# A scheduled two-stage MLP kernel on one core: x0 and x1 joined in one load, single-tile groups up to tile 5, and another load, PE and helper order

## Chip, core and metric

The kernel runs on one core of a Trainium2 chip. The time is the device time of one execution in microseconds (us); lower is better. A core has a tensor engine (PE, with PEld for its weight loads), a vector engine (DVE), a scalar engine (ACT), GpSimd (POOL) and a sync engine (SP). DMAs are issued here from SP and from ACT, each with its own ring, and run on the core's 16 DMA engines.

## What is computed

x is one sequence of S = 2048 tokens with D = 512 channels, F is 1792, everything is bf16. From the reference:

```python
    h = _gelu(_layernorm(x, axis=-1) @ w1)
    c = D // 4
    g0 = jnp.pad(h[:, :, 0*c:1*c], ((0, 0), (1, 0), (0, 0)))[:, :S, :]
    g1 = jnp.pad(h[:, :, 1*c:2*c], ((0, 0), (0, 1), (0, 0)))[:, 1:, :]
    g2 = jnp.pad(h[:, :, 2*c:3*c], ((0, 0), (2, 0), (0, 0)))[:, :S, :]
    g3 = jnp.pad(h[:, :, 3*c:   ], ((0, 0), (0, 2), (0, 0)))[:, 2:, :]
    hs = jnp.concatenate([g0, g1, g2, g3], axis=-1) @ w2
    x1 = x + hs
    h2 = _gelu(_layernorm(x1, axis=-1) @ w3) @ w4
    return x1 + h2
```

The four quarters of h are shifted along the sequence by +1, -1, +2 and -2 tokens, so token tile t of hs needs h of tiles t-1, t and t+1.

## The kernel before, in words

The sequence is cut into 16 tiles of 128 tokens. Layer 1 normalises x and multiplies by w1 (`up1`), GELU puts h, transposed, into `hT`; `mix` multiplies four shifted slices of `hT` by w2 and DVE adds x to give x1. Layer 2 normalises x1, multiplies by w3 (`up2`), GELU gives `h2T`, and `down` multiplies by w4; DVE adds x1 and a DMA stores the tile. A layer-2 tile t carries the number q = 16 + t in the tables, so `ty:16` is the transposition of layer-2 tile 0.

A tile's normalisation (`ln`, lines 384 to 465) is a chain of small steps: statistics on DVE (`bnst`, line 416, and `bnag`, line 418) or, for the tiles in `STAT_ACT`, on ACT (`sum`, line 395, `ssq`, line 400, with `msq` and `vpe` on DVE, lines 408 and 412); then the reciprocal root on POOL (`rstd`, line 423); then the normalisation itself on the engine that `NORM` names (DVE, line 445; ACT, line 454; POOL, line 457; the last two need `nmr`, line 450, on the engine that `NMR` names). The normalised tile is then transposed, by PE for the tiles named `sa`, `sb`, `ty` in the script (line 490, with a copy from PSUM, line 498, on the engine that `EVAC` names) and by a DMA transpose from SP (line 463) for the other 24. Tile 0 goes another way (`NAT`): centred only, split into two halves, multiplied with the tokens as rows (`ra`, `rb`, line 528), GELU with the scale (line 569), and h transposed by PE (`th`, line 594) and copied by the engine in `HEV` (line 604).

`GROUPS` says how many neighbouring tiles one `up` step takes together: a group of n tiles streams n*128 columns for each weight block (`mm_up`, line 626, GELU at line 641). `mix` is line 666 with its residual at lines 673 and 677; `down` is line 695 with its residual at line 703.

What sets the order: PE executes `SCRIPT` from left to right, exactly. Loads are issued in the order of `LOADS`, an item marked `@act` on the ACT ring, all others on SP (lines 368 and 377; `x4-5` is one DMA for two tiles, `w1a` and `w1b` are the halves of w1; a `tp` item for a tile that PE transposes has no effect). All other work is put in order by the planner `Program.order` and `place`: it computes a due time for each operation back from the script, starting at `DUE`, adds `BIAS`, and simulates the engines and rings with fixed durations, `HOP` and `LAG`. Each engine then executes its list in order, so that a waiting instruction holds everything behind it on its engine. `y_ps` has three buffers, used in rotation by `up` and the PE transposes, `o_ps` has two, used by `mix`, `down`, `th` and the warm-up. Before anything has landed PE runs a number of matmuls on zeros (`warm`, line 720).

Of the kernel before, what the change touches and what calls it, by code (L numbers as in the profile page):

```python
# [25 lines left out]
class Program:  # L26
# [2 lines left out]

    HOP = {"pe": 200.0, "dve": 155.0, "act": 220.0, "pool": 120.0, "sp": 70.0}  # L30
    LOOK = {"dve": 300.0, "act": 300.0}
    DUE = 164483.0
    BEGIN = {"sp": 30.0, "act": 150.0, "pe": 400.0, "dve": 150.0, "pool": 450.0}
    ENTRY = 1900.0
    COLD, RESTART = 4300.0, 800.0
    LAG = {"load": 750, "tp": 700}

    def __init__(self):
        self.ops = []
# [12 lines left out]
    def order(self):  # L52
# [58 lines left out]
        assert seen == len(self.ops), "cycle"  # L111
        if self.DUE:

            topo, left = [], [len(d) for d in preds]
            stack = [i for i, n in enumerate(left) if n == 0]
            while stack:
                i = stack.pop()
                topo.append(i)
                for j in succs[i]:
                    left[j] -= 1  # L120
                    if left[j] == 0:
                        stack.append(j)
            due, t = {}, self.DUE
            for op in self.ops:
# [12 lines left out]
        for op in self.ops:  # L137
            op.prio += BIAS.get(op.name, 0.0)
            if op.first is not None:
# [11 lines left out]
    def place(self, succs, order_only):  # L151
# [46 lines left out]
        def land(op):  # L198
            nonlocal moved, last
            if op.queue == "tp":  # L200
                at = max(clock + 500.0, op.start + 2450.0, last + 600.0) + self.LAG["tp"]
            elif op.name.startswith("out"):
                at = clock + 300.0
                self.total = max(self.total, at)
            else:
                moved += op.dur
                at = clock + 600.0 + min(600.0, 0.3 * moved) + (600.0 if op.dur > 1400.0 else 0.0)
                at += self.LAG["load"] if moved > 1200.0 else 50.0
            if op.queue != "tp":
# [47 lines left out]
        self.seq = out  # L257
        return out

GROUPS = {1: (1, 1, 1, 1, 2, 1, 4, 2, 2, 1), 2: (2, 4, 4, 2, 4)}  # L260
NORM = {0: "act", 3: "act", 7: "pool", 8: "act", 9: "pool", 10: "pool", 11: "pool", 12: "pool", 14: "act", 15: "act", 16: "pool", 18: "act", 19: "act", 24: "pool", 25: "act", 26: "pool", 27: "pool", 29: "pool", 30: "pool", 31: "act"}
EVAC = {0: "both", 1: "both", 2: "both", 4: "both", 8: "both", 9: "dve", 10: "dve", 11: "dve", 12: "dve", 13: "dve", 14: "dve", 16: "dve", 17: "dve", 19: "both", 20: "both", 21: "both", 22: "both", 23: "both", 24: "dve", 25: "both", 27: "both", 29: "both", 30: "both", 31: "both"}
STAT_ACT = (0, 7, 9, 12, 13, 15, 18, 21, 25, 29, 30)
TAIL = (256, 160, 96)
NMR = {0: "pool", 1: "pool", 3: "pool", 5: "pool", 6: "pool", 7: "pool", 8: "pool", 9: "pool", 11: "pool", 13: "pool", 14: "pool", 15: "pool", 16: "pool", 17: "pool", 18: "pool", 20: "pool", 21: "pool", 22: "pool", 26: "pool", 27: "pool", 28: "pool", 29: "pool", 31: "pool"}
NAT = (0,)
SPLIT = (0,)
CSPLIT = ()
HEV = {0: "dve", 4: "dve"}
BIAS = {}  # L270
LOADS = """
x1 x2 tp2 x0@act w1a w1b x3 x4-5 tp5 w2a w2b x6-7 w3 tp17 w4a x8-10 w4b tp6 x11-12 tp1 tp16 x13-15
"""
SCRIPT = """
warm:9 sa:0 sb:0 ty:1 ra:0 rb:0 ty:2 up1:1 th:0 up1:2 mix:0 ty:3 ty:5 mix:1 ty:4 up1:3-4 ty:16 mix:2 ty:17
mix:3 up2:0 mix:4 up1:5 down:1 down:0 mix:5 up1:6-7 mix:8 mix:6 up1:9 mix:9-10 up1:8 mix:7 mix:11 up2:1
mix:13 mix:15 up2:3 down:5 mix:12 up2:2 mix:14 down:2 down:4 down:3 down:6-8 down:11 down:9 up2:4 down:10
down:12-15
"""

def bass_standalone__mixer_s_mlp__prompt_kernel(nc, x, w1, w2, w3, w4, out):
# [3 lines left out]
    NT, DC, FC = S // P, D // P, F // P  # L285
    groups = {l: [(sum(GROUPS[l][:i]), n) for i, n in enumerate(GROUPS[l])] for l in GROUPS}
    NXN, NO, NPAIR, NOB, NJ = 16, 4, 3, 2, 4
# [8 lines left out]
    with ExitStack() as es:  # L296
# [87 lines left out]
        def ln(layer, t):  # L384
# [3 lines left out]
            col = lambda a: a[:, q : q + 1]  # L388
            how = NORM.get(q, "dve")
            sign = -1.0 if q in NAT and how == "act" else 1.0  # L390
            if q in STAT_ACT:
                if layer == 1:
# [22 lines left out]
            else:  # L415
# [4 lines left out]
                       writes=[(("mv", q), 0), (("vpe", q), 0)], dur=75)  # L420
            var = vpe[:, q : q + 1] if q in STAT_ACT else mv[:, q, 1:2]
            pg.add("pool", f"rstd{q}",
# [3 lines left out]
            if q in NAT:  # L426
                assert how != "act" or q in STAT_ACT

# [18 lines left out]
            else:  # L447
                eng = NMR.get(q, "dve")
                pg.add(eng, f"nmr{q}",
# [17 lines left out]
        def pe_transpose(t, q, pair):  # L467
            layer = 1 if q < NT else 2
            how = EVAC.get(q, "act")
            if pair:  # L470
# [104 lines left out]
        def h_transpose(t):  # L575
            g = group_of[1, t]
            how = HEV.get(t, "act")
            k = NAT.index(t)
# [71 lines left out]
        def mm_mix(t):  # L650
# [20 lines left out]
            wr = [(("x1", t), 0)]  # L671
            if NT + t in STAT_ACT:
                f = lambda e: e.scalar_tensor_tensor(x1_sb[:, t, :], dst, 1.0, x_sb[:, t, :], ALU.mult, ALU.add,  # L673
# [198 lines left out]
```

## Time and profile before

| | |
|---|---|
| time, median of 5 runs | 135.45 us (135.12 to 135.84) |
| the profiled execution | 135.84 us, of which the span of the trace is 134.5 us and 1.34 us lie around it |
| granted TensorE clock | 1.000 |
| busy share of the span: PE, PEld | 98%, 53% |
| busy share: ACT, DVE, POOL | 43%, 38%, 22% |
| chain that ended last | PE 94%, DMA 4%, SP's queue 1% |
| loads on SP (issue start, time to landing) | x1 0.1, 2.4; x2 0.6, 2.6; w1a 1.0, 4.8; w1b 1.5, 5.0; w4b 9.9, 11.5 |
| load on ACT | x0 0.2, 2.6 |
| DMA transposes | 24, median 1.27 us to issue, 2.5 us to landing |

The table of busy times tells how full an engine is over the whole span. The chain is read back from the last instruction: at each step it names what the step was waiting for, so it shows what set the time. The timeline gives start, duration, engine, line and operation; in brackets stands how long the engine had been idle and what ended that. Matmul durations in the timeline overlap, because matmuls are pipelined; the chain's pieces do not.

### The profile page before, as it was taken

To read this page: it belongs to the slowest core of one execution; us is meant where nothing else is said; L and a number is where in the kernel's file an instruction comes from. 1 tells how busy PE (TensorE), PEld (TensorE's weight loads), DVE (VectorE), ACT (ScalarE), POOL (GpSimd) and SP (SyncE) were. 2 spreads that over 40 slices of the span, in tenths; PEclk is the share of its full clock that TensorE was granted. 3 is DMA by queue.
4 is the path that set the end of the run, shared out by engine and by line. 5 is a ranking of instruction groups with operands and counts; after the bars stand their busy time and mean duration, and the time that the engine had idled before them with its cause. 6 is when DMAs were issued, how large, how long until landed. Compare 5 with 4: busy or idle time off the path is not lost.

```text
span 134.5 us, 2014 instructions
## 1 busy us (share of the span) xinstructions
PE 131.4 (98%) x789; PEld 71.4 (53%) x789; DVE 50.8 (38%) x134; ACT 58.4 (43%) x92; POOL 29.7 (22%) x68
## 2 busy tenths in 40 slices
PE   8799999999999999999999999999999999999994
PEld 3287687644666444478544444444444444444464
DVE  2689986856178930070061004232222200012222
ACT  5789349989544275547315554000000155520000
POOL 2444549892102860006010001200000000000000
DMA  4999999455452134100411000211111100001112
GB/s 134 301 386 396 350 299 239 90 80 115 82 116 78 34 73 95 39 0 1 82 39 39 0 0 0 70 47 44 39 39 57 60 0 0 0 5 39 39 39 78
DMA packets 21289, 12.19 MB, mean 91 GB/s; under 512 B 13856, under 2 KB 20768, under 8 KB 21280
## 3 DMA queue, kind: packets, MB, share of 16 engines
q1 hardware_dynamic: 20704, 11.80, 32.8%
q10 hardware_dynamic: 576, 0.26, 0.7%
q8 instruction: 6, 0.10, 0.3%
q14 instruction: 3, 0.02, 0.1%
HBM read 6.82 MB, written 2.10 MB: 66 GB/s over the span
## 4 chain that ended last, share of the span: by engine, by line
PE 94%; DMA 4%; SPq 1%; issue 0%; DVE 0%
PE y_ps L626 46%; PE o_ps L695 36%; PE o_ps L666 10%; DMA w_sb<-in_w_dram 4%; PE y_ps L490 1%; SPq L368 1%; PE y_ps L528 0%; SPq L377 0%; DVE o_sb L703 0%; PE o_ps L594 0%; SPq L857 0%
## 5 line engine op out<-in xcount | busy, mean ns | idle before, releaser
L626 PE MATMUL y_ps<-xnT,w_sb 128*128 128x512 bf16 (+2 forms) x424 | 63.6, 309 | 0.0
L626 PEld LDWEIGHTS y_ps<-xnT,w_sb 128*128 128x128 bf16 x424 | 38.3, 98 | 24.9
L641 ACT ACTIVATE h2T<-y_ps 128x1024 bf16<-128x1024 f32 (+1 forms) x29 | 28.6, 994 | 48.8 <-PE y_ps L626 48.6
L695 PE MATMUL o_ps<-w_sb,h2T 128*128 128x512 bf16 (+3 forms) x252 | 49.1, 355 | 0.0
L695 PEld LDWEIGHTS o_ps<-w_sb,h2T 128*128 128x128 bf16 x252 | 23.6, 98 | 24.7
L703 DVE TENSOR_TENSOR o_sb<-o_ps,x_sb 128x512 bf16<-128x512 f32 (+3 forms) x18 | 11.4, 632 | 46.9 <-PE o_ps L695 46.9
L423 POOL TENSOR_TENSOR rstd<-mv,neghalf 128x1 f32<-128x1 f32 x21 | 11.5, 549 | 23.6 <-DVE mv L418 14.2
L666 PE MATMUL o_ps<-w_sb,hT 128*128 128x512 bf16 x64 | 15.8, 379 | 0.0
L416 DVE BATCH_NORM_STATS2 st<-x_sb 128x6 f32<-128x512 bf16 x21 | 14.1, 678 | 3.5 <-DMA x_sb<-in_x_dram 3.4
L423 POOL TENSOR_TENSOR rstd<-vpe,neghalf 128x1 f32<-128x1 f32 x11 | 6.0, 547 | 29.3 <-DVE vpe L412 29.2
L673 DVE SCALAR_TENSOR_TENSOR x_sb<-o_ps,x_sb 128x512 bf16<-128x512 f32 x5 | 3.4, 686 | 19.2 <-PE o_ps L666 19.2
L641 ACT ACTIVATE hT<-y_ps 128x512 bf16<-128x512 f32 (+1 forms) x10 | 8.1, 807 | 5.4 <-PE y_ps L626 5.3
L677 DVE TENSOR_TENSOR x_sb<-o_ps,x_sb 128x512 bf16<-128x512 f32 x11 | 7.6, 687 | 4.2 <-PE o_ps L666 4.0
L666 PEld LDWEIGHTS o_ps<-w_sb,hT 128*128 128x128 bf16 x64 | 6.0, 98 | 5.8
L457 POOL TENSOR_SCALAR xn_buf<-x_sb,rstd,nmr 128x512 bf16<-128x512 bf16 x11 | 8.4, 765 | 0.8 <-DVE nmr L450 0.4
L400 ACT ACTIVATE junk<-x_sb 128x512 bf16<-128x512 bf16 x11 | 6.9, 624 | 2.2 <-DVE x_sb L673 2.2
L454 ACT ACTIVATE xn_buf<-x_sb,nmr,rstd 128x512 bf16<-128x512 bf16 x8 | 6.3, 806 | 0.8 <-POOL nmr L450 0.7
L445 DVE TENSOR_SCALAR xn_buf<-x_sb,mv,rstd 128x512 bf16<-128x512 bf16 x12 | 5.3, 443 | 2.9 <-POOL rstd L423 2.6
L720 PE MATMUL o_ps<-zeros 128*128 128x512 bf16 x9 | 4.0, 626 | 0.4 <-DVE zeros L347 0.4
L395 ACT ACTIVATE junk<-x_sb 128x512 bf16<-128x512 bf16 x6 | 3.7, 624 | 0.7 <-DMA x_sb<-in_x_dram 0.7
L418 DVE BATCH_NORM_AGGREGATE mv<-st 128x2 f32<-128x9 f32 x21 | 3.8, 189 | 0.3
L450 POOL TENSOR_SCALAR nmr<-mv,rstd 128x1 f32<-128x1 f32 x13 | 3.4, 263 | 0.7
(34 smaller groups left out, 28.4 us busy)
## 6 DMA issues: line engine op xcount, KB each, us to landing
out_dram<-o_sb SPq DMA_DIRECT2D x15, 128.0 KB, 1.7
w_sb<-in_w_dram SPq DMA_DIRECT2D x1, 1792.0 KB, 10.0
w_sb<-in_w_dram SPq DMA_DIRECT2D x2, 896.0 KB, 11.7
w_sb<-in_w_dram SPq DMA_DIRECT2D x4, 256.0 KB, 5.2
x_sb<-in_x_dram SPq DMA_DIRECT2D x3, 256.0 KB, 5.2
x_sb<-in_x_dram SPq DMA_DIRECT2D x2, 384.0 KB, 9.1
x_sb<-in_x_dram SPq DMA_DIRECT2D x3, 128.0 KB, 2.6
xnT<-xn_buf SPq DMA_TRANSPOSE x24, 2.5
```

The costliest lines, as they stand in the source:

```text
L400: (lambda d: (lambda e: e.activation(d, src, ACT_F.Square, accum_out=sums[:, q, 1:2])))(junk[:, b, :]),
L416: pg.add("dve", f"bnst{q}", lambda e: e.bn_stats(st9[:, q, 0:6], src), reads=rs, writes=[(("st", q), 0)], dur=605)
L423: lambda e: e.tensor_tensor(col(rstd), var, neghalf[:], ALU.pow),
L445: lambda e: e.tensor_scalar(dst, src, mv[:, q, 0:1], rstd[:, q : q + 1], ALU.subtract, ALU.mult),
L454: f = lambda e: e.activation(dst, src, ACT_F.Identity, bias=nmr[:, q : q + 1], scale=rstd[:, q : q + 1])
L457: f = lambda e: e.tensor_scalar(dst, src, rstd[:, q : q + 1], nmr[:, q : q + 1], ALU.mult, ALU.add)
L626: ins = e.matmul(y_ps[:, p, W * i : W * (i + 1)], wsb[:, dc, P * fc : P * (fc + 1)], src[:, dc, P * t0 : P * t0 + W], start=(dc == 0), sto ...
L641: (lambda d, s: (lambda e: e.activation(d, s, ACT_F.Gelu_apprx_tanh)))(dst, ysrc),
L666: ins = e.matmul(dst, hT[:, j, c0 : c0 + P], w2_sb[:, j, :], start=(j == 0), stop=(j == DC - 1))
L677: f = lambda e: e.tensor_tensor(x1_sb[:, t, :], dst, x_sb[:, t, :], ALU.add)
L695: ins = e.matmul(dst, h2T[:, fc, P * t : P * (t + 1)], w4_sb[:, fc, cs], start=(fc == 0), stop=(fc == FC - 1))
L703: (lambda d, c: (lambda e: e.tensor_tensor(o_sb[:, oi, c], d, x1_sb[:, t, c], ALU.add)))(dst, cs),
```

## The change

It touches tables only; no function is altered. x0 and x1 become one DMA on SP, and ACT issues no load. Layer-1 groups before: tiles 0, 1, 2, 3 alone, 4-5, 6 alone, 7-10, 11-12, 13-14, 15 alone. After: tiles 0 to 5 alone, 6-9, 10 alone, 11-12, 13 alone, 14-15. One warm-up matmul is added. The loads after x4-5 come in another order, most of x as single tiles, and no DMA transpose stands between loads. The tables of engines for the helpers, the planner's `DUE`, `LAG` and `BIAS`, and the order of PE's script are others.

```diff
-    DUE = 164483.0
+    DUE = 94375.3
...
-    LAG = {"load": 750, "tp": 700}
+    LAG = {"load": 450, "tp": 700}
...
-GROUPS = {1: (1, 1, 1, 1, 2, 1, 4, 2, 2, 1), 2: (2, 4, 4, 2, 4)}
-NORM = {0: "act", 3: "act", 7: "pool", 8: "act", 9: "pool", 10: "pool", 11: "pool", 12: "pool", 14: "act", 15: "act", 16: "pool", 18: "act", 19: "act", 24: "pool", 25: "act", 26: "pool", 27: "pool", 29: "pool", 30: "pool", 31: "act"}
-EVAC = {0: "both", 1: "both", 2: "both", 4: "both", 8: "both", 9: "dve", 10: "dve", 11: "dve", 12: "dve", 13: "dve", 14: "dve", 16: "dve", 17: "dve", 19: "both", 20: "both", 21: "both", 22: "both", 23: "both", 24: "dve", 25: "both", 27: "both", 29: "both", 30: "both", 31: "both"}
-STAT_ACT = (0, 7, 9, 12, 13, 15, 18, 21, 25, 29, 30)
+GROUPS = {1: (1, 1, 1, 1, 1, 1, 4, 1, 2, 1, 2), 2: (2, 4, 4, 2, 4)}
+NORM = {0: "act", 4: "pool", 9: "pool", 11: "pool", 12: "pool", 13: "pool", 14: "pool", 15: "act", 19: "pool", 20: "pool", 21: "act", 22: "act", 23: "act", 25: "act", 28: "pool", 29: "act", 31: "act"}
+EVAC = {0: "dve", 2: "both", 3: "dve", 8: "both", 9: "dve", 10: "both", 11: "both", 13: "dve", 15: "dve", 16: "both", 17: "dve", 18: "dve", 20: "both", 22: "dve", 27: "both", 29: "both", 30: "dve", 31: "both"}
+STAT_ACT = (0, 5, 7, 8, 9, 13, 21, 22, 28, 30)
...
-HEV = {0: "dve", 4: "dve"}
-BIAS = {}
+HEV = {0: "dve", 1: "dve", 3: "dve", 4: "dve", 6: "dve"}
+BIAS = {"bnag14": -172.25, "bnag2": -591.918, "bnag28": -353, "bnst6": 1934.91, "msq0": -541.481, "ssq4": -586, "vpe0": -295.453, "vpe9": 895}
 LOADS = """
-x1 x2 tp2 x0@act w1a w1b x3 x4-5 tp5 w2a w2b x6-7 w3 tp17 w4a x8-10 w4b tp6 x11-12 tp1 tp16 x13-15
+x0-1 x2 w1a w1b x3 tp17 tp4 x4-5 w2b w2a x8 tp4 w3 tp17 x10 x9 tp1 x7 x6 w4a w4b x15 x12 x14 tp0 x11 x13
 """
 SCRIPT = """
-warm:9 sa:0 sb:0 ty:1 ra:0 rb:0 ty:2 up1:1 th:0 up1:2 mix:0 ty:3 ty:5 mix:1 ty:4 up1:3-4 ty:16 mix:2 ty:17
-mix:3 up2:0 mix:4 up1:5 down:1 down:0 mix:5 up1:6-7 mix:8 mix:6 up1:9 mix:9-10 up1:8 mix:7 mix:11 up2:1
-mix:13 mix:15 up2:3 down:5 mix:12 up2:2 mix:14 down:2 down:4 down:3 down:6-8 down:11 down:9 up2:4 down:10
-down:12-15
+warm:10 sa:0 sb:0 ty:1 ra:0 rb:0 ty:2 up1:1 th:0 up1:2 ty:3 mix:0 up1:3 mix:1 ty:4 mix:2 ty:5 up1:4 ty:16
+up1:5 ty:17 mix:3 up2:0 mix:4 down:1 up1:6 down:0 mix:5 up1:8 up1:7 mix:6-7 up1:9 mix:9 mix:8 up1:10 mix:10
+up2:1 mix:11 mix:15 up2:2 mix:12 down:2 down:4 mix:14 up2:3 mix:13 down:3 down:6-7 up2:4 down:10-11 down:8
+down:14 down:5 down:9 down:12-13 down:15
 """
```

`NMR` changes in the same manner (fewer entries on POOL); `TAIL`, the split of the last tile's `down` into 256, 160 and 96 columns, stays. What the planner makes of the tables, engine by engine, is fixed when the program is built: in the first 17 us DVE then runs `bnst3 ev2dve bnag3 bnst4 norm3 evh0 bnag4 msq5 ev3 vpe5 x1_0 bnst16 norm5 x1_1 bnag16 bnst17 norm16 bnag17 x1_2 norm17 ev16dve msq8 vpe8 ev17`, ACT runs `gelur0 ev2act sum5 gelu1_1 ssq5 gelu1_2 sum8 ssq8 gelu1_3 ev4 ev5 gelu1_4 ev16act sum7 gelu1_5`, and SP issues all loads and then `tp8 tp7 tp6 tp9 tp10 ...`. (`ev` is the copy of a transposed tile, `evh0` that of tile 0's h, `x1_t` the residual after `mix:t`, `gelu1_g` the GELU of `up1:g`.)

More of the change, by code (lines that the diff above doesn't have):

```diff
@@ L258, in place @@
         return out
-GROUPS = {1: (1, 1, 1, 1, 2, 1, 4, 2, 2, 1), 2: (2, 4, 4, 2, 4)}
-NORM = {0: "act", 3: "act", 7: "pool", 8: "act", 9: "pool", 10: "pool", 11: "pool", 12: "pool", 14: "act", 15: "act", 16: "pool", 18: "act", 19: "act", 24: "pool", 25: "act", 26: "pool", 27: "pool", 29: "pool", 30: "pool", 31: "act"}
-EVAC = {0: "both", 1: "both", 2: "both", 4: "both", 8: "both", 9: "dve", 10: "dve", 11: "dve", 12: "dve", 13: "dve", 14: "dve", 16: "dve", 17: "dve", 19: "both", 20: "both", 21: "both", 22: "both", 23: "both", 24: "dve", 25: "both", 27: "both", 29: "both", 30: "both", 31: "both"}
-STAT_ACT = (0, 7, 9, 12, 13, 15, 18, 21, 25, 29, 30)
+GROUPS = {1: (1, 1, 1, 1, 1, 1, 4, 1, 2, 1, 2), 2: (2, 4, 4, 2, 4)}
+NORM = {0: "act", 4: "pool", 9: "pool", 11: "pool", 12: "pool", 13: "pool", 14: "pool", 15: "act", 19: "pool", 20: "pool", 21: "act", 22: "act", 23: "act", 25: "act", 28: "pool", 29: "act", 31: "act"}
+EVAC = {0: "dve", 2: "both", 3: "dve", 8: "both", 9: "dve", 10: "both", 11: "both", 13: "dve", 15: "dve", 16: "both", 17: "dve", 18: "dve", 20: "both", 22: "dve", 27: "both", 29: "both", 30: "dve", 31: "both"}
+STAT_ACT = (0, 5, 7, 8, 9, 13, 21, 22, 28, 30)
 TAIL = (256, 160, 96)
-NMR = {0: "pool", 1: "pool", 3: "pool", 5: "pool", 6: "pool", 7: "pool", 8: "pool", 9: "pool", 11: "pool", 13: "pool", 14: "pool", 15: "pool", 16: "pool", 17: "pool", 18: "pool", 20: "pool", 21: "pool", 22: "pool", 26: "pool", 27: "pool", 28: "pool", 29: "pool", 31: "pool"}
+NMR = {0: "pool", 4: "pool", 5: "pool", 6: "pool", 7: "pool", 10: "pool", 14: "pool", 15: "pool", 16: "pool", 17: "pool", 18: "pool", 19: "pool", 20: "pool", 22: "pool", 25: "pool", 27: "pool", 28: "pool", 31: "pool"}
 NAT = (0,)
```

## The prediction

> **What bounds the kernel now.** I read the chain that ended last first. Its pieces are start, duration, what:
>
> ```profile
> 1.49 4.99 DMA w_sb<-in_w_dram
> 6.48 0.05 issue
> 6.53 0.60 PE y_ps L528 x2
> 7.13 0.22 PE y_ps L490 x4
> 7.36 0.89 PE y_ps L626 x16
> ...
> 9.39 0.94 PE o_ps L666 x4
> ...
> 24.58 6.04 PE o_ps L695 x28
> ...
> 117.53 15.19 PE o_ps L695 x98
> 132.72 0.02 issue
> 132.74 0.26 DVE o_sb L703
> ```
>
> The second half of w1 (`w1b`, issued at 1.49) lands at 6.48. From 6.53 to 132.72 every piece is PE with no gap between: 126.19 us of matrix work. After it come one DVE addition and the last store (134.5 − 132.72 = 1.8). The waits of PE say the same; columns are total, times, longest:
>
> ```profile
> PE y_ps L528 <- ACT xnT L498: 0.8, 1, 0.8
> PE o_ps L720 <- DVE zeros L347: 0.4, 1, 0.4
> ```
>
> Both lie ahead of 6.53. So the time is three terms: the wait for w1 (6.53), PE's work (126.19), the tail (1.8), and 1.34 around the span: 135.84, the profiled execution, 0.39 above the median of 135.45. A helper engine matters only where it makes PE wait.
>
> Why w1b takes 4.99 us is seen in short stretches of the DMA. Last columns: DMA share, GB/s.
>
> ```profile
> 2.00:2.50 0.50, 0.50 (x2) 0.15 (x1) 0.00 (x1) 0.11 (x1) 0.00 (x0) 1.00 1.02 352
> 2.50:3.00 0.50, 0.50 (x3) 0.17 (x2) 0.50 (x1) 0.16 (x1) 0.00 (x0) 1.00 0.95 127
> 3.00:3.50 0.50, 0.50 (x3) 0.23 (x2) 0.47 (x3) 0.50 (x2) 0.00 (x0) 1.00 0.31 70
> 3.50:4.00 0.50, 0.50 (x3) 0.06 (x1) 0.49 (x1) 0.47 (x2) 0.49 (x1) 1.00 0.53 82
> 4.00:4.50 0.50, 0.50 (x4) 0.14 (x2) 0.40 (x2) 0.50 (x2) 0.06 (x1) 1.00 0.95 326
> ```
>
> x0 to x2 (393 KB) move at 350 GB/s; then, with w1 already issued, the rate falls to 70 to 127 for 1.5 us and comes back. In the hole 140 KB move, which at 350 take 0.4 us: about 1.1 us are lost.
>
> **PE's own work.** Behind the warm-up only the grouping changes; 24 tiles are transposed by DMA and 8 by PE in both. Before has five single layer-1 groups at line 626 (tile 0 goes by line 528), three doubles and one of four; after has seven singles, two doubles and one of four. So one double becomes two singles: a single is 0.89 us, a double 1.75 (the chain's piece at 41.03), and 2 × 0.89 − 1.75 = +0.03. `down`, with its tail of three pieces, stays.
>
> **The tenth warm-up.** Nine take 3.97 us, one starts every 0.43, so the tenth would move the first transposes from 4.25 to about 4.69. Tile 0's copies, now both on DVE (0.29 each, behind bnst2, norm1 and bnag2, which end at about 4.95), end near 5.2 and 5.5. They are needed when w1a and w1b land, 5.81 and 6.48. Cost nothing; without that cover up to 0.4.
>
> **x0 and x1 in one load.** Before, x1 lands at 2.49, x0 at 2.84. Joined on SP, the same 256 KB, started at the same 0.1, should land when the later did, 2.84; tile 0 loses nothing, tile 1 0.35, which is the 4.95 above. If it lands later, w1 covers about 0.5 us (5.5 + 0.5 against 6.48 less the hop), beyond that one for one. SP issues four DMAs up to w1b as before, with about 0.43 each (w1a, also two rows per partition, took 0.43), and the same 896 KB are ahead of w1b's end.
>
> Here a rule speaks against any gain. The Trainium skill, "DMA: Bandwidth & Descriptors", section "Issuing engines are not separate DMA queues", says that DMAs of several issuing engines run on the same 16 engines and interleave, and that a second issuer saves only the sequencer's issue time. By it, dropping the ACT ring moves w1b by 0: 6.48 stays. The row with the hole allows the other reading: the hole begins as ACT's x0 runs out, and if the change of rings makes it, one ring closes it and w1b lands near 5.4; then tile 0's copy (5.5, plus a hop of 0.1) decides, and rows start their second half at 5.6 instead of 6.53: −0.9. The trace cannot tell: all slow packets in the hole belong to SP's queue (w1a), which speaks for the rule. I take 0, with −0.9 and +0.3 (one ring fetching two loads where two rings did) as ends.
>
> The tail now makes the ACT ring's first DMA. On unused rings x1 (SP) took 2.40 and x0 (ACT) 2.63 beside it, so 0 to +0.2; I take 0. ACT's missing issue (0.38 us at 0.21) only advances its table load, nothing waits there.
>
> **The order of the first 17 us.** I lay the new script on the chain's durations, from rows ending at 7.13: ty:2 7.36, up1:1 8.25, th:0 8.47, up1:2 9.39, ty:3 9.61, mix:0 10.47, up1:3 11.36, mix:1 12.22, ty:4 12.45, mix:2 13.31, ty:5 13.53, up1:4 14.42, ty:16 14.64, up1:5 15.53, ty:17 15.75, mix:3 16.61. Then each wait, with the trace's durations:
>
> - ACT: gelur0 7.24, ev2act 7.82, sum5 8.2, gelu1_1 8.82 to 9.42 (sum5 is new ahead of it, 0.62); mix:0 needs it at 9.61: spare 0.1. Next ssq5, gelu1_2 from 9.94, sum8, ssq8, gelu1_3 11.68 to 12.28; mix:2 needs it at 12.45: spare 0.1. x5 must land by 8.2 (before: 7.7) and x8 by 10.4; x8 comes where x6 did (x6-7 landed at 9.9).
> - DVE and POOL for tile 16: x1_1 12.26 to 12.95, bnag16 to 13.15, rstd16 (0.55) to 13.78, norm16 (0.41) to 14.27; ty:16 at 14.42: spare 0.1.
> - Tile 17, in line behind that: bnst17 13.05 to 13.72, norm16, bnag17 to 14.38, rstd17 to 15.0, norm17 15.09 to 15.49; ty:17 at 15.53: spare 0.04.
>
> The pieces of that chain, as the trace before has them (start, duration):
>
> ```profile
> 11.36 0.69 DVE L416 BATCH_NORM_STATS2 st<-x_sb 128x6 f32<-128x512 bf16 x1
> ...
> 12.42 0.55 POOL L423 TENSOR_TENSOR rstd<-mv,neghalf 128x1 f32<-128x1 f32 x1 [1.50 <-DVE mv L418]
> 13.07 0.26 POOL L450 TENSOR_SCALAR nmr<-mv,rstd 128x1 f32<-128x1 f32 x1
> 13.43 0.76 POOL L457 TENSOR_SCALAR xn_buf<-x_sb,rstd,nmr 128x512 bf16<-128x512 bf16 x1
> ```
>
> So PE fits everywhere, but five times with 0.04 to 0.1 to spare. Before was also tight (its first mix took 0.94 against 0.86 later). I take +0.1 for small stalls, ends 0 and +0.9.
>
> **Loads and transposes later.** Ahead of w3's end stand 128 KB fewer (x8 instead of x6 and x7), so it lands 0.36 before the 14.5 of now (4.5 + 10.0); needed at 16.6, spare 2.4. w4b ends with the same bytes ahead, 21.4 or earlier, since no transpose interrupts the loads; down:1 needs it at 23.58. What is late next is group 6-9: up1:6 now stands ahead of down:0 and mix:5, at 26.6, before it was at 31.5. Its four transposes queue on SP behind all loads, whose issue should be over by 17 (tp6 kept SP from 15.84 to 17.95 before, and x11 to x15 were issued after it). norm9, the last, ends about 21.2 (POOL, after vpe9, nmr9); with 1.27 us per issue tp9 goes out at 22.1 and lands 2.5 to 4.7 later, 24.6 to 26.8. I take no stall, at most 0.2. Layer 2 has room: mix:5 ends at 33.9 and up2:1 needs its tile at 43.5; mix:13 ends near 84, up2:4 needs it at 93.
>
> **Sum.** 135.84 + 0.03 + 0.1 = 135.97 for an execution like the profiled one, so 135.6 beside the median of 135.45.
>
> **Rivals.** Within 0.3% (135.04 to 135.86) is what a measurement cannot tell from no change.
>
> - No change, 135.6, chance 0.40: the start stays with w1b, the stalls remain small. For it: the 126.19 us of PE are untouched and every helper fits.
> - Earlier start, 134.8, chance 0.27: the hole closes. 0.9 is the most, since tile 0's chain takes over, and the tight chains behind it give back some 0.2: 135.45 − 0.9 + 0.2 + 0.03. For it: the hole follows the end of the two-ring stretch. Against: slow packets of w1 itself.
> - Slower, 136.3, chance 0.33: the in-order helpers no longer fit under PE. The place is tile 17's chain from mix:1 to ty:17, 3.27 us of helpers against 3.31 us of PE work; in the trace before mix:1 ended at 11.65 and ty:17 began at 15.62, 3.97 us. It decides as soon as one DVE step more (0.2 to 0.7 us) gets into the chain, or one x load holds DVE; the same delay moves ev17 and up2:0. One bnst (0.69) at that place: 135.6 + 0.7. Against: the sum above has no such step in it.
>
> A change that does nothing at all is the first case with its two small terms left out, 135.45.
>
> The range holds the first case with its ends and most of the others: 134.7 to 136.4. The first case's own range is 135.2 to 135.9. The chances: faster 0.27, within 0.3% 0.40, slower 0.33.
>
> **What would show it.** Right: w1b again lands near 6.5 and the same DMA hole stands at 2.5 to 4.0; rows of line 528 end at 7.1; PE's waits behind that sum to under 0.3; up1:6 (line 626, 512 columns) begins near 26.7. Earlier start: no hole, L528's second half before 6.0. Slower: PE or PEld waits on DVE's or ACT's `xn_buf`, `xnT` or `hT` between 9 and 17. The forecast is wrong if the joined load lands after 3.4, or tp9 after 26.7.

## The result and the profile after

The changed kernel takes 136.25 us in the median against 135.59 for the kernel before: a ratio of 1.0052, 95% interval 1.004 to 1.0064. It is slower by some 0.7 us, just outside what the prediction called no change. The runs also scatter more: 135.66 to 137.29, before 135.12 to 136.06. The profiled execution took 136.25, its span is 134.9 (before 134.5). Medians and ratios, here and below, leave out runs that took over 1.5% more than the fastest of the same kernel: one each in three of the experiments.

The chain that ended last, of the changed kernel, around 22 us and at its end (start, duration, what):

```profile
21.26 0.76 POOL xn_buf L457
22.02 0.04 issue
22.06 0.46 POOL rstd L423
22.52 4.33 DMA xnT<-xn_buf
26.86 0.14 issue
26.99 3.61 PE y_ps L626 x16
30.60 3.02 PE o_ps L695 x14
...
105.88 27.28 PE o_ps L695 x154
133.16 0.02 issue
133.19 0.26 DVE o_sb L703
```

Before, this chain left PE only once, at w1b. Now it leaves PE at 26.99, through a DMA transpose issued at 22.52, back to tile 9's normalisation on POOL (line 457). That normalisation (`norm9`) ended at 22.02. SP was then still held by the issue of tile 6's transpose, from 21.20 to 22.48, so that SP's own line stood ahead of the issue at 22.52 as well. From 26.99 on PE is again without a gap; the tail is 1.7 us as it was.

PE's waits, of the changed kernel (total, times, longest):

```profile
PE o_ps L720 <- DVE zeros L347: 0.4, 1, 0.4
PE y_ps L626 <- DMA xnT<-xn_buf: 0.3, 1, 0.3
```

The wait ahead of line 528 is no longer in this list, and one for a transpose has come. Its 0.3 is less than the loss, since the ends of the matmuls in the profile are modelled and overlap the wait. Starts of neighbouring blocks show the whole of it. PE's timeline of the changed kernel:

```profile
14.31 1.06 PE L626 MATMUL y_ps<-xnT,w_sb 128*128 128x128 bf16 x16
15.33 0.40 PE L490 MATMUL y_ps<-ident,xn_buf 128*128 128x128 bf16 x4
...
22.54 1.03 PE L666 MATMUL o_ps<-w_sb,hT 128*128 128x512 bf16 x4
23.48 3.18 PE L695 MATMUL o_ps<-w_sb,h2T 128*128 128x512 bf16 x14
26.99 3.61 PE L626 MATMUL y_ps<-xnT,w_sb 128*128 128x512 bf16 x16 [0.33 <-DMA xnT<-xn_buf]
```

- down:1 starts at 23.48 and is 3.02 long; up1:6 starts 3.51 later. Lost: 0.49.
- up1:5 starts at 14.31 and is 0.89 long; ty:17 starts 1.02 later. Lost: 0.13.
- mix:4 starts at 22.54 and is 0.86 long; down:1 starts 0.94 later. Lost: 0.08.

Those are 0.70. Add 0.03 for the two single groups and take off 0.08 for the small waits that the kernel before had and this one does not: PE's stretch from the second half of line 528 to its end grows by 0.65, from 126.19 to 133.16 − 6.32 = 126.84. The start is 0.21 earlier (6.32 for 6.53), which leaves 0.44, the 0.4 between the two spans.

The DMA stretches that answer to those of before (last columns: DMA share, GB/s):

```profile
2.50:3.00 0.50, 0.50 (x3) 0.19 (x2) 0.00 (x0) 0.00 (x0) 0.00 (x0) 1.00 0.72 225
3.00:3.50 0.50, 0.50 (x3) 0.23 (x2) 0.39 (x1) 0.39 (x1) 0.00 (x0) 1.00 0.79 57
3.50:4.00 0.50, 0.50 (x3) 0.19 (x2) 0.47 (x3) 0.47 (x3) 0.00 (x0) 1.00 0.41 68
4.00:4.50 0.50, 0.50 (x3) 0.01 (x1) 0.50 (x2) 0.50 (x2) 0.38 (x1) 1.00 0.65 174
```

The hole behind the first three tiles is there with a single ring too. The joined load lands at 3.1 (issue 0.1, 3.0 to landing).

### The profile page after: what moved, and what is told of

Same layout as the page of the kernel before. It is cut to its first block, busy times and chain, and to the rows that moved or that the text cites. A ratio compares the mean times of both kernels' runs of the same rounds, so it can differ in the third digit from the quotient of the medians.

```text
span 134.9 us, 2047 instructions
## 1 busy us (share of the span) xinstructions
PE 132.1 (98%) x806; PEld 71.7 (53%) x806; DVE 51.7 (38%) x136; ACT 57.1 (42%) x89; POOL 27.6 (20%) x62
## 4 chain that ended last, share of the span: by engine, by line
PE 79%; DMA 11%; SPq 3%; POOL 2%; ACT 1%; DVE 1%; issue 1%
PE y_ps L626 38%; PE o_ps L695 34%; DMA x_sb<-in_x_dram 7%; PE o_ps L666 7%; DMA xnT<-xn_buf 3%; SPq L368 2%; POOL rstd L423 1%; SPq L377 1%; ACT junk L395 1%; POOL xn_buf L457 1%; DVE st L416 0%; ACT junk L400 0%; ACT hT L641 0%; DVE o_sb L703 0%; DVE nmr L450 0%
## 5 line engine op out<-in xcount | busy, mean ns | idle before, releaser
L641 ACT ACTIVATE h2T<-y_ps 128x1024 bf16<-128x1024 f32 (+1 forms) x29 | 28.5, 991 | 23.5 <-PE y_ps L626 23.4
L695 PEld LDWEIGHTS o_ps<-w_sb,h2T 128*128 128x128 bf16 x252 | 23.5, 98 | 25.3 <-DVE st L416 0.4
L423 POOL TENSOR_TENSOR rstd<-mv,neghalf 128x1 f32<-128x1 f32 x22 | 12.3, 562 | 30.9 <-DVE mv L418 29.8
L416 DVE BATCH_NORM_STATS2 st<-x_sb 128x6 f32<-128x512 bf16 x22 | 14.7, 676 | 3.3 <-DMA x_sb<-in_x_dram 3.1
L677 DVE TENSOR_TENSOR x_sb<-o_ps,x_sb 128x512 bf16<-128x512 f32 x12 | 8.2, 684 | 14.1 <-PE o_ps L666 14.1
L423 POOL TENSOR_TENSOR rstd<-vpe,neghalf 128x1 f32<-128x1 f32 x10 | 5.5, 551 | 27.1 <-DVE vpe L412 27.1
L400 ACT ACTIVATE junk<-x_sb 128x512 bf16<-128x512 bf16 x10 | 6.3, 626 | 10.6 <-DVE x_sb L673 10.6
L445 DVE TENSOR_SCALAR xn_buf<-x_sb,mv,rstd 128x512 bf16<-128x512 bf16 x15 | 6.5, 434 | 5.9 <-POOL rstd L423 5.5
L673 DVE SCALAR_TENSOR_TENSOR x_sb<-o_ps,x_sb 128x512 bf16<-128x512 f32 x4 | 2.8, 692 | 11.4 <-PE o_ps L666 11.4
L457 POOL TENSOR_SCALAR xn_buf<-x_sb,rstd,nmr 128x512 bf16<-128x512 bf16 x9 | 6.9, 767 | 0.5 <-DVE nmr L450 0.4
L454 ACT ACTIVATE xn_buf<-x_sb,nmr,rstd 128x512 bf16<-128x512 bf16 x7 | 5.6, 809 | 3.2 <-DVE nmr L450 2.9
L395 ACT ACTIVATE junk<-x_sb 128x512 bf16<-128x512 bf16 x6 | 3.8, 630 | 2.4 <-DMA x_sb<-in_x_dram 2.3
L490 PE MATMUL y_ps<-ident,xn_buf 128*128 128x128 bf16 x32 | 3.3, 220 | 0.1
(34 smaller groups left out, 26.7 us busy)
```

The costliest lines, as they stand in the source:

```text
L400: (lambda d: (lambda e: e.activation(d, src, ACT_F.Square, accum_out=sums[:, q, 1:2])))(junk[:, b, :]),
L416: pg.add("dve", f"bnst{q}", lambda e: e.bn_stats(st9[:, q, 0:6], src), reads=rs, writes=[(("st", q), 0)], dur=605)
L423: lambda e: e.tensor_tensor(col(rstd), var, neghalf[:], ALU.pow),
L445: lambda e: e.tensor_scalar(dst, src, mv[:, q, 0:1], rstd[:, q : q + 1], ALU.subtract, ALU.mult),
L454: f = lambda e: e.activation(dst, src, ACT_F.Identity, bias=nmr[:, q : q + 1], scale=rstd[:, q : q + 1])
L457: f = lambda e: e.tensor_scalar(dst, src, rstd[:, q : q + 1], nmr[:, q : q + 1], ALU.mult, ALU.add)
```

## Experiments

All but one part of each kernel is held: a list of operation names fixes every engine's order as the planner made it for the kernel the experiment starts from, so that an edit moves only what it names. Theory A, formed from the profile, is that up1:6, pulled 5 us forward, waits for the last DMA transpose of tiles 6 to 9. Theory B is the place that the prediction's slower rival named: the helper chains ahead of 17 us.

**down:0 ahead of up1:6.** PE's script and nothing else; up1:8 goes ahead of mix:5 too, to cover the GELU of up1:6:

```diff
-up1:5 ty:17 mix:3 up2:0 mix:4 down:1 up1:6 down:0 mix:5 up1:8 up1:7 ...
+up1:5 ty:17 mix:3 up2:0 mix:4 down:1 down:0 up1:6 up1:8 mix:5 up1:7 ...
```

> The changed kernel with one part of PE's order put back: down:0 runs ahead of up1:6, and up1:8 ahead of mix:5 to cover up1:6's GELU; the helpers' orders are held as they were. Theory A (the last DMA transpose of tiles 6 to 9, landing at 26.9, makes PE wait 0.5 us ahead of up1:6 in the profiled execution): up1:6 is then due 3 us later, at about 29.4, the wait is gone, the time falls by 0.5 to 0.7 us to about 135.6, no slower than before, and the runs scatter less. Theory B (the 0.66 us lie in the helper chains ahead of 17 us, the place the prediction named): up1:6 never mattered, the time stays at 136.2.

135.55 us, ratio to the kernel before 0.9999 (0.9987 to 1.0011); the interval does not touch that of the changed kernel. The runs lie between 135.22 and 135.92. That they scatter less than the changed kernel's is weak evidence by itself, since the kernel before, run 67 times beside this one, reached 136.96. PE's timeline of this kernel:

```profile
22.22 1.03 PE L666 MATMUL o_ps<-w_sb,hT 128*128 128x512 bf16 x4
23.16 6.20 PE L695 MATMUL o_ps<-w_sb,h2T 128*128 128x512 bf16 x28
29.20 5.36 PE L626 MATMUL y_ps<-xnT,w_sb 128*128 128x512 bf16 x32
```

up1:6 follows two down steps after 6.04 = 2 × 3.02, with no wait, although tile 9's transpose landed only at 28.5 here. The small waits of theory B are still in this trace (ty:17 1.02 after up1:5, down:1 0.94 after mix:4), and the time is back at the old one. Theory A stands: the order of PE's steps around up1:6 makes up the difference.

This profile also shows that the issue does not follow the normalisation alone: `norm9` ended at 20.8 here, 1.2 earlier than in the changed kernel's profile, and the transpose still went out at 22.7, right behind tile 6's, whose issue held SP from 21.15 to 22.69.

**Tile 9's transpose later.** SyncE's order and nothing else:

```diff
-tp8 tp7 tp6 tp9 tp10 tp11
+tp8 tp7 tp6 tp10 tp9 tp11
```

> The changed kernel with the suspected wait made larger: tile 9's transpose is issued behind tile 10's, which cannot go before 24.4. Theory A (up1:6 waits for the last of its four transposes): it lands near 28, 1.2 us later than in the changed kernel, and the time rises by the same 1.0 to 1.4 us to about 137.4. Theory B (the loss is in the helper chains ahead of 17 us): at most 0.3 us more.

138.2 us (137.49 to 139.41), ratio 1.0218 (1.017 to 1.0266). In its profile the transpose goes out at 25.8, lands at 28.3, and up1:6 starts at 28.40: 1.41 later than in the changed kernel, and the span is 136.4, 1.5 longer. A larger wait gives a longer time. The median rose by 1.95, more than the 1.0 to 1.4 expected, but only four runs stand behind it. In the longest, 139.41, the granted clock was 0.988 instead of 1.000; the middle of the other three is 137.7, a rise of 1.45. The profiled execution, with a clock of 1.000, has a second wait:

```profile
PE o_ps L666 <- DMA w_sb<-in_w_dram: 1.2, 1, 1.2
PE y_ps L626 <- DMA xnT<-xn_buf: 0.7, 1, 0.7
```

mix:0 waited 1.2 for w2, which landed at 9.5 and 10.2 here and at 8.2 and 8.9 in the changed kernel's profile, with the same loads ahead. But PE then waited for the transpose anyway, so those 1.2 us are not in the sum a second time. What the rest of the 1.95 comes from is not shown.

**x9, x7, x6 ahead of w3.** Why is the transpose late?

```diff
-x8 w3 x10 x9 x7 x6 w4a
+x8 x9 x7 x6 w3 x10 w4a
```

> The changed kernel with x9, x7 and x6 loaded ahead of w3 instead of behind it, all orders held. It tells apart why tile 9's transpose is late. Theory A1 (its normalisation is late, because ACT waits 0.9 us for x7 at 16.08 and everything behind it, ssq9, rstd9, norm9, slips): norm9 ends near 21.2, its transpose is issued about 0.9 us sooner and lands near 26.0; the wait goes, the time falls by 0.4 to 0.6 us to about 135.7. Theory A2 (the transposes queue behind the loads and then follow each other at about 1.2 us, whatever the normalisation does): tile 9 still lands near 26.8 and the time stays at 136.2. w3 lands about 1.1 us later, near 14.9, and is needed at 16.4: no cost in either.

136.24 us, ratio 1.0039 (1.002 to 1.0058): as the changed kernel. Tile 9 is normalised from 20.40 on instead of 21.26, its transpose goes out at 21.8 instead of 22.5 and lands at 26.2 instead of 26.9. The 0.86 us gained in the normalisation bring 0.7 at the landing, and the last load landed 0.7 earlier too (22.76 for 23.45). In this profile up1:6 did not wait (26.68 after 23.66, 3.02). What PE gained there, and by an early w1, it had lost further ahead:

```profile
7.84 1.07 PE L626 MATMUL y_ps<-xnT,w_sb 128*128 128x128 bf16 x16 [0.21 <-DVE xnT L498]
9.09 0.40 PE L490 MATMUL y_ps<-ident,xn_buf 128*128 128x128 bf16 x4 [0.18 <-DVE xn_buf L445]
```

Here w1b had landed at 5.6, but x3 not before 6.9, and VectorE's fixed order keeps tile 2's copy (line 498) behind x3's statistics. An earlier w1 is then given back at x3. The median speaks against A1, but this profile cannot tell issue from queue, since both moved by 0.7; the next run does.

**The transposes ahead of the last five loads of x.** SyncE's order:

```diff
-w4a w4b x15 x12 x14 x11 x13 tp8 tp7 tp6 tp9 tp10
+w4a w4b tp8 tp7 tp6 tp9 x15 x12 x14 x11 x13 tp10
```

> The changed kernel with only SyncE's order altered: the transposes of tiles 8, 7, 6, 9 are issued ahead of the last five loads of x instead of behind them. Theory A2 (the four transposes are late because they queue behind the last loads; in three profiles tile 9's lands 3.4 us after the last load has landed, whenever it was issued): they then follow w4b alone, some 1.8 us sooner, tile 9's lands near 25.0 to 25.5, the wait ahead of up1:6 goes and the time falls to about 135.6. Theory A1 (tile 9's own normalisation is what is late): issue at 22.1 to 22.5 and landing stay, the time stays at 136.2. A third outcome: the five x tiles, now landing near 26, hold VectorE in its fixed order and cost as much elsewhere.

140.21 us, ratio 1.0353 (1.0318 to 1.0388): the third outcome. What it was made for is shown first: tile 9's transpose, issued at 22.6, nearly the same moment as in the changed kernel, lands at 25.1, 2.5 us later instead of 4.3, and up1:6 starts 3.02 after down:1. The line of SP's transpose issued at 22.6:

```profile
DMA to landing us min/median/max: 2.5/2.5/2.5
```

So 1.8 us of the landing come from the loads ahead of it: A2. The price lies elsewhere; PE's waits and its timeline of this kernel:

```profile
PE o_ps L666 <- ACT hT L641: 3.6, 1, 3.6
PE o_ps L695 <- DVE x_sb L677: 1.5, 1, 1.5
```

```profile
23.23 3.18 PE L695 MATMUL o_ps<-w_sb,h2T 128*128 128x512 bf16 x14
26.25 3.62 PE L626 MATMUL y_ps<-xnT,w_sb 128*128 128x512 bf16 x16
31.33 3.19 PE L695 MATMUL o_ps<-w_sb,h2T 128*128 128x512 bf16 x14 [1.46 <-DVE x_sb L677]
38.08 1.02 PE L666 MATMUL o_ps<-w_sb,hT 128*128 128x512 bf16 x3 [3.56 <-ACT hT L641]
```

VectorE waits in its fixed order for x12 and x11 (until 26.58 and 29.39), behind which stands the residual of mix:4 that frees down:0's PSUM buffer; then ScalarE waits 4.3 us for tile 15's normalisation, behind which stands the GELU that mix:5 needs. Moving loads behind the transposes without moving the helpers that use them costs some 4 us net where 0.5 was to be saved.

**Rings.** The kernel before with the joined load, and the changed kernel without it:

```diff
-x1 x2 tp2 x0@act w1a
+x0-1 x2 tp2 w1a
```

> The kernel before with x0 and x1 joined in one load on the SyncE ring, nothing else changed, all orders held. Theory A (one ring brings w1 sooner: in the changed kernel w1b landed at 6.27, before at 6.48): w1b lands near 6.25 and the time falls by 0.2 us, ratio about 0.9985. Theory B (the rule that one or two issuing engines make no difference; the 0.2 us are chance in one profile): ratio 1.000, w1b near 6.5. Theory C (the joined load, landing at 3.1 instead of 2.5 and 2.8, holds tile 0 or 1): slower by 0.1 to 0.3.

```diff
-x0-1 x2 w1a
+x1 x2 x0@act w1a
```

> The changed kernel with only the joined load undone: x1, x2 on SyncE and x0 on ScalarE as before, all orders held. Theory A (one ring brings w1 0.2 us sooner): 0.2 us slower than the changed kernel, 136.45 against 136.25, w1b near 6.5. Theory B (no difference between rings): 136.25, w1b near 6.3. The late transposes ahead of up1:6 don't depend on it, so the wait there stays near 0.5 us in either case, less any time by which the start comes later.

The first gives 135.73, ratio 1.0003 (0.9981 to 1.0026): no difference within 0.3%. The second gives 135.91, 1.0028 (1.001 to 1.0045), which overlaps the changed kernel's 1.004 to 1.0064; if anything it is faster, the opposite of what theory A there wanted. By medians the joined load is slower both times (135.73 beside 135.52 for the kernel before in the same series, 136.25 for 135.91), which would fit theory C, a cost of 0.1 to 0.3 us; the intervals neither show nor exclude it. It is not what makes the changed kernel slow, for down:0 first has the joined load too and is at 0.9999. w1b landed at 5.7 in both profiles, once on one ring, once with two. The wait ahead of up1:6 is 0.42 in the second (26.59 after 23.15), as expected unaffected.

**The kernel before and the changed kernel once more**, same programs, one execution and profile each.

> The kernel before once more, same program, for one further profile: does w1b's landing vary by itself? If the landing at 6.48 was chance, it differs here by some tenths, as it does among the four runs with the changed loads (5.6, 5.8, 5.8, 5.6); if two rings cause it, it is again near 6.5.

> The changed kernel once more, same program, for one further profile. Theory A2 (the transposes of tiles 6 to 9 trail the loads): tile 9's lands about 3.4 us after the last load of x has landed, near 26.5, as in three profiles so far, and PE waits ahead of up1:6 for what is left after its own progress, 0.3 to 0.7 us. If the landing falls elsewhere against the last load, the 3.4 us were chance.

The kernel before: 135.72, w1b at 6.4. The changed kernel: 137.66, a span of 136.3, w1b at 6.6; tile 9's transpose went out at 22.8 and landed at 28.2, 5.5 later and 4.5 after the last load. PE's waits, and two rows of its timeline:

```profile
PE y_ps L626 <- DMA xnT<-xn_buf: 1.4, 1, 1.4
PE y_ps L528 <- DMA w_sb<-in_w_dram: 0.5, 1, 0.5
```

```profile
23.78 3.18 PE L695 MATMUL o_ps<-w_sb,h2T 128*128 128x512 bf16 x14
28.37 3.61 PE L626 MATMUL y_ps<-xnT,w_sb 128*128 128x512 bf16 x16 [1.42 <-DMA xnT<-xn_buf]
```

The 3.4 us behind the last load were not a constant. But this shows where a wide scatter can come from: the same program, the same wait, 1.6 us lost (28.37 − 23.78 − 3.02) instead of 0.49. How often an execution falls this way is not shown.

**Both repairs.** down:0 first, and VectorE's `bnag16` ahead of `norm5`, `bnag17` ahead of `norm16`.

> The changed kernel with down:0 ahead of up1:6 (as in e1_down0_first) and, besides, VectorE's order around tiles 16 and 17 mended: bnag16 ahead of norm5 and bnag17 ahead of norm16. ty:17 came 0.13 us late in every profile of the changed order. If that wait is on the path, it goes and the time is 0.1 us below e1_down0_first, 135.4, just below the kernel before. If another wait takes its place (x3's landing when w1 comes early, w1 itself), it stays at 135.5.

135.57 us, ratio 1.0011 (1.0 to 1.0023). In its profile ty:17 follows up1:5 after 0.89, the 0.13 is gone, while ty:16 now starts 0.97 after up1:4 instead of 0.89. The gain of 0.1 us that was hoped for does not show; no version here beats the kernel before.

## Why the prediction was right or wrong, by its steps

The forecast was 135.6, no change; the measured 136.25 lies in the range, but outside the first case's own 135.2 to 135.9, in the region of the slower case. The mechanism of that case was not the one at work, so that the range holds the result by luck. Three of the prediction's own signs say the same: it was to be wrong if tile 9's transpose landed after 26.7, and it landed at 26.86; up1:6 was to begin near 26.7 and began at 26.99; PE's waits behind the start were to stay under 0.3 and, by the starts of the blocks, came to 0.70.

- **w1 and the ring: value right.** It took 0 for the ring against −0.9 and +0.3. The hole is there on one ring, so the reading that two rings make it is refuted. w1b's landing moves by itself: 6.5, 6.4, 5.7 with two rings, 6.3, 5.6, 5.7, 5.6, 5.6, 6.0, 6.3, 6.6 with one, over all the profiles. The 0.21 of the changed kernel's start cannot be told from that. The rule that the prediction weighed (the Trainium skill, "DMA: Bandwidth & Descriptors", "Issuing engines are not separate DMA queues": a second issuing engine saves only the time of issuing) fits the ratio 1.0003, within 0.3%.
- **Joined load: nearly.** It landed at 3.1 instead of 2.84, and tile 0's copies ended at 5.4 and 5.7 instead of 5.2 and 5.5. In the profile w1b, at 6.28, covers this, as said.
- **PE's own work, tenth warm-up, ACT ring in the tail: right.** From 26.99 on there are 106.17 us of PE, and the sum of the pieces of before gives 126.19 + 0.03 − 0.60 (line 528) − 19.47 (the schedule from 7.13 to 26.60) = 106.15; the tail did not grow.
- **The first 17 us: size right.** 0.13 at ty:17, where 0.04 was to spare, and nothing at the other three places (the prediction counts five places in all and lists four) in the changed kernel's profile; +0.1 had been allowed. The case of 136.3 that rested on this chain did not happen.
- **Group 6-9: the step that failed.** It said that tile 9's transpose "goes out at 22.1 and lands 2.5 to 4.7 later, 24.6 to 26.8. I take no stall, at most 0.2". It went out at 22.5 and 22.8 in the two profiles of the changed kernel, landed 4.3 and 5.5 later, and cost 0.49 and 1.6 us. The new deadline, 26.6, was found and the upper end reached it; the error was to take the stall from the favourable end. Nor was the upper end the worst on view: in the trace before, tile 6's transpose, issued at 15.8 behind loads that had not landed, took 6.0. Tile 9's took 4.3 to 5.8 us in the six profiles in which it went out before the last load had landed, and 2.5 in the two in which all loads ahead had landed (the transposes ahead of the loads: 22.6 after 21.6; tile 9's later: 25.8 after 23.5). That step carries the result: without it (down:0 first) the time is 0.9999 of before.

The issue itself slipped by 0.4. The prediction has no term for x7, which landed at 16.05; ScalarE waited for it 0.9 us, and the chain through ssq9, rstd9 and norm9 ended at 22.0 instead of 21.2. Tile 7's normalisation ended at 19.9, its transpose went out at 20.0, tile 6's at 21.2 and tile 9's at 22.5, one issue of 1.2 to 1.3 us behind the other. As x9, x7, x6 ahead of w3 showed, loading x7 sooner brings nothing measurable.

What stays open: why a transpose behind loads takes 4.3 in one execution and 5.5 in another, what makes w1b's landing move by 1 us, and whether the joined load costs a tenth or two.

## What to carry to other kernels

When a change pulls a step forward on a full engine, take its new start as a deadline for each transfer it reads, and price each transfer from rows issued into an equally full queue, not by the median of the run. If the deadline falls inside the range of those landings, count a stall, and allow for scatter as well: a step with no slack can turn the varying landing of a DMA into varying time. Moving an independent step of PE in between (here down:0, 3 us) took the wait away, where pulling transfers forward through the shared queue starved the fixed orders behind it.

## What the runs showed of the hardware beyond that

- A DMA transpose issued at 22.5 behind loads still in flight took 4.3 us to land, one issued at 22.6 with only transposes still in flight ahead of it 2.5. Between the loads' last bytes and the next transposes the DMA engines moved little: 44 and 23 GB/s in the two half microseconds from 22.0 to 23.0 of the changed kernel, with three transposes issued and not landed. In its second profile, where the transpose took 5.5, this stretch lasted three half microseconds (43, 25 and 19 GB/s from 22.0 to 23.5).
- One program's first weights land at times that differ by tenths to 1 us from execution to execution (w1b 5.6 to 6.6 over the eleven profiles, with the same bytes ahead). In each of them the rate falls behind the first 390 KB: from 305 to 379 GB/s between 2.0 and 2.5 us to 57 to 205 in the slowest half microsecond before 4.0. In the three with w1b at 5.6 the rate from 2.5 to 4.5 was 233 to 255 in the mean, in the five with 6.3 or later 131 to 225.
- PE does not gain all of an early landing: with w1b 0.7 us earlier, the span was 134.1 instead of 134.4 (down:0 first, without and with the second repair). In the former x3, landed at 6.4, held VectorE, and ty:3 started 1.06 after up1:2 instead of 0.89.
